# One pair of PSUM banks shared by decoded words and attention in the first group of a fused attention and expert kernel

## The chip, the cores and the metric

The kernel runs on one core of a Trainium2 chip. A core has five engines that run side by side and wait for each other by semaphores: TensorE (PE in the profile; PEld is its loading of weights), VectorE (DVE), ScalarE (ACT), GpSimd (POOL) and SyncE (SP, which here issues transfers). Matrix products land in PSUM, a small memory of banks; everything else is worked on in SBUF. The metric is the device time of one execution in microseconds (us), as the median of three runs.

## The reference

Three blocks follow each other. Chunks of 64 positions attend to themselves; the result, 4608 rows of 512, goes through a dense layer pair with `h - tanh(h)`; then each row is sent to two of eight experts, whose outputs are weighted and added.

```
scores = scale * q_c @ k_c.T        # chunks of 64, per head
attn   = exp(scores - max) / (sum + 1e-9)
x      = attn @ v_c                 # -> 4608 x 512
h = x @ w_in ; x = (h - tanh(h)) @ w_out          # 512 -> 2048 -> 512
top2 of x @ w_gate + log1p(exp(x @ w_noise)) * noise
out += weight * (max(x @ w1[e], 0) @ w2[e])       # for both experts of a row
```

The weights `w_in` and `w_out` reach the kernel as 64-bit floats, which the chip reads as pairs of 32-bit words; they have to be turned into 32-bit floats first. All other inputs are 32-bit floats.

## The kernel before

**Tiles and groups.** The rows are 36 tiles of 128, in nine groups of four. Group g's dense layer takes 16 steps (f = 0 to 15). A step is one block of layer 1 (`hp`, line 338, 12 matmuls of 128x512) and one block of layer 2 (`acc`, line 446, 12 matmuls), the latter a step behind, so the TensorE alternates `hp(f)`, `acc(f-1)`. Between blocks there are slots, two to a step: slot 2f stands behind `hp(f)`, slot 2f+1 behind `acc(f-1)`. Slots hold everything else in a list that is filled before (`at(h, fn)`), and what is in one slot is issued in the order in which it was put there: attention first, then the work on weights. Every engine works its own instructions strictly in that order.

**Attention of a tile** goes through scores (`s_mm`, 16 matmuls of 64x64), a maximum and a difference on the VectorE (`mx`, `e`), the exponential on the ScalarE, a sum and a reciprocal (`sm`, function `u_e`) with a multiplication, a transposition by the TensorE (`u_t`, `pt`), products with v (`p_mm`), and a split of the result in two parts, `xt` (ScalarE, then VectorE). The multiplication is done by the GpSimd for tiles below 8 and by the VectorE for the others (line 187). While group 0 runs its dense layer, the four tiles of group 1 (tiles 4 to 7) are attended to in its slots; from group 1 on the tiles of the next group, in "visits" that each transpose one tile, multiply the one before and score the one after (`u_attn`).

**Decoding.** In group 0 alone, the weights are still being prepared: in slot 2f the block of `w_in` for step f+2, in slot 2f+1 that of `w_out` for step f+1. The VectorE makes each in three instructions (lines 307, 313, 315) over a half-finished word, `word`, that is kept in PSUM; the third writes `x` to SBUF. Then the ScalarE and the GpSimd split `x` into `wa` or `wb`.

**PSUM.** Two banks are `hp` (and `pt`), four are `acc`, and two are left. Before, while decoding runs, one of the two is `word` and the other is `one`; `one` holds the scores or the products of a tile. The 16 matmuls of a tile are of two halves (`c`), and `u_s_chunk` and `u_p_chunk` do half a tile, 8 matmuls, in a slot of its own. At the end of group 0 (`decoded`) the two banks become `pair`, of shape [128, 2, 512]; a whole tile's scores lie in half 1 of both banks (columns 256 to 511) and products in half 0.

Of the kernel before, what the change touches and what calls it, by code (L numbers as in the profile page):

```python
# [31 lines left out]
def moe_chain_kernel(ctx: ExitStack, tc: tile.TileContext, q, k, v, w_in, w_out, wgn, noise,  # L32
# [27 lines left out]

    early, decoding = ExitStack(), ExitStack()
    ep = early.enter_context(tc.tile_pool(name="ep", bufs=1, space=PSUM))
    pairs = [ep.tile([128, 2, 512], F32, name=f"pair{i}") for i in range(3)]
    pools = {}
# [2 lines left out]
    def first_step():  # L69
        early.close()  # L70
        pools["acc"] = ctx.enter_context(tc.tile_pool(name="ap", bufs=1, space=PSUM))
        pools["two"] = decoding.enter_context(tc.tile_pool(name="gp", bufs=1, space=PSUM))

    def decoded():
        decoding.close()
        pools["two"] = ctx.enter_context(tc.tile_pool(name="qp", bufs=1, space=PSUM))
        pools["pair"] = pools["two"].tile([128, 2, 512], F32, name="pair")

    def after(what, n):
        turn[what] += 1  # L80
# [31 lines left out]
    def load_q(i):  # L112
        Q[i] = spare("wa", NF1 - 2)[:, i % 2] if 2 <= i < GS[0] else blk("q", "q", 2)
        nc.sync.dma_start(Q[i], q[i])
# [17 lines left out]
    def place_of(i, half):  # L132
        banks = pairs[after("early", 3)] if i < GS[0] else pools["pair"]
        return banks[:, :, 256 * half:256 * half + 256].rearrange("p c (a t) -> p c a t", a=4)
# [3 lines left out]
    def products(out, lhs, rhs, chunks=(0, 1)):  # L138
        for h in range(0, 8, 2):
            for c in chunks:  # L140
                rows = slice(64 * c, 64 * c + 64)
                for o in range(2):
                    cols = slice(64 * h + 64 * o, 64 * h + 64 * o + 64)
                    nc.tensor.matmul(out[64 * o:64 * o + 64, c, h // 2, :], lhsT=lhs[rows, cols],  # L144
                                     rhs=rhs[rows, cols], start=True, stop=True,
                                     tile_position=(64 * c, 64 * o))
# [53 lines left out]
        nc.scalar.copy(PT[i], pt)  # L200

    def p_mm(i):
        PX[i] = place_of(i, 0)
        products(PX[i], V.pop(i), PT.pop(i))
        if GS[0] <= i + 2 < NT:
            load_v(i + 2)
# [16 lines left out]
        p_lo(i)  # L223

    def one_bank():
        p = pools["two"].tile([128, 512], F32, name="one", bufs=1)
        return p.rearrange("p (c a t) -> p c a t", c=2, a=4)

    def u_s_chunk(i, c):
        if c == 0:
            PS[i] = one_bank()
            MX[i] = sp.tile([128, 2, 4, 1], F32, name="mx", bufs=2)
            Et[i] = sp.tile([128, 8, 64], F32, name="e", bufs=2)
        products(PS[i], Q[i], K[i], (c,))
        ps, mx = PS[i][:, c], MX[i][:, c]
        nc.vector.reduce_max(mx, ps, axis=AX.X)
        nc.vector.tensor_tensor(Et[i].rearrange("p (a c) t -> p c a t", c=2)[:, c], ps,
                                mx.to_broadcast([128, 4, 64]), op=ALU.subtract)  # L240
        if c == 1:
            for d in (Q, K, PS, MX):
                d.pop(i)
            load_q(i + 2)
            load_k(i + 2)

    def u_p_chunk(i, c):
        if c == 0:
            PX[i] = one_bank()
        products(PX[i], V[i], PT[i], (c,))  # L250
        g, j = place[i]
        if i == G0[g] and c == 0:
            XT[g] = new_xt(g, 128 * GS[g])
        s0 = j * 128 + 64 * c
        hi, lo = [XT[g][:, b, :, s0:s0 + 64] for b in range(2)]
        nc.scalar.copy(hi, PX[i][:, c])
        nc.vector.tensor_tensor(lo, PX[i][:, c], hi.bitcast(F32), op=ALU.subtract)
        if c == 1:
            for d in (V, PT, PX):
                d.pop(i)  # L260
            load_v(i + 2)

    def u_attn(old, mid, new):
        for t, fn in ((mid, u_t), (old, p_mm), (new, s_mm), (old, p_split), (new, s_max),
# [29 lines left out]
    def decode(raw, early=False, half=False):  # L294
        if raw.dtype == F32:
            return None if half else raw
        raw = raw.rearrange("p (m s) -> p m s", s=2)
        lo, hi = raw[:, :, 0], raw[:, :, 1]

        if early:  # L300
            part = pp.tile([128, 512], U32, name="word", tag="hp", bufs=2)
        else:
            if "two" in pools:
                part = pools["two"].tile([128, 512], U32, name="word", bufs=1)
            else:
                part = pairs[2][:, 0].bitcast(U32)
        nc.vector.tensor_scalar(part, lo, 29, None, op0=ALU.logical_shift_right)
        return part if half else decode_rest(raw, part)

    def decode_rest(raw, part):  # L310
        hi = raw[:, :, 1]
        x = blk("x", "y", 4, U32)
        nc.vector.scalar_tensor_tensor(part, hi, 3, part, op0=ALU.logical_shift_left,  # L313
                                       op1=ALU.bitwise_or)
        nc.vector.scalar_tensor_tensor(x, hi, 0x80000000, part, op0=ALU.bitwise_and,
                                       op1=ALU.bitwise_or)
        return x.bitcast(F32)

# [728 lines left out]
    def at(h, fn, *a):  # L1047
        slots[h].append(L(fn, *a))

    for i, hs in zip(range(GS[0], sum(GS[:2])), ((2, 3, 4, 5, 8, 15, 17), (5, 6, 7, 8, 11, 19, 20),  # L1050
                                                 (9, 11, 12, 13, 18, 22, 24),
                                                 (12, 14, 15, 16, 21, 26, 28))):
        at(hs[0], u_s_chunk, i, 0)
        at(hs[1], u_s_chunk, i, 1)
        at(hs[2], u_x, i)
        at(hs[3], u_e, i)
        at(hs[4], u_t, i)
        at(hs[5], u_p_chunk, i, 0)
        at(hs[6], u_p_chunk, i, 1)

    n0 = sum(GS[:2])
    visits = []
    at(H1, decoded)
    for g in range(1, NG - 1):
        hs = (1, 5, 9, 13, 18, 24) if g == 1 else (5, 9, 13, 24)
        for h in hs:
            visits.append((H1 * g + h, n0 if n0 < NT else None))
            n0 += 1  # L1070
    flow = [None, None]
    for h, i in visits:
        at(h, u_attn, *flow, i)
        if i:
            at(h + 1, u_x, i)
            at(h + 2, u_e, i)
        flow = [flow[1], i]

    for g in range(NG):
        h0 = H1 * g  # L1080
        at(h0, load_nz, g)
        if g > 0:
            n = GS[g - 1]
            for j in range(n):
                i = G0[g - 1] + j
                at(h0 + 1 + j, u_z, i)
                at(h0 + 5 + j, u_yt, i)

            if g == NG - 1:
                hs = (9, 11, 12, 13, 15, 17, 17, 19, 20, 23)  # L1090
            elif g == 1:
                hs = (9, 13, 14, 16, 17, 19, 21, 21, 22, 24)
            else:
                hs = (9, 13, 14, 16, 17, 18, 19, 20, 20, 24)
            for h, fn in zip(hs, (u_lg, u_gate, u_gate2, u_gate2h, u_gate2a, u_gate2b, u_gate2m,
                                  u_gate2c, u_gate3, u_pos)):
                at(h0 + h, fn, g - 1)
        if g == 0:
            at(26, store_consts)
            for o, f in ((0, 3), (1, 2), (1, 3)):  # L1100
                at(0, fetch_w, o, f)
            for f in range(NF1):
                at(2 * f, fetch_w, 0, f + 4)
                at(2 * f, prep_w, 1, f)
                at(2 * f, decode_w, 0, f + 2)
                at(2 * f, rebias_w, 0, f + 3)
                at(2 * f + 1, fetch_w, 1, f + 4)
                at(2 * f + 1, prep_w, 0, f + 2)
                at(2 * f + 1, decode_w, 1, f + 1)
                at(2 * f + 1, rebias_w, 1, f + 2)  # L1110
        else:
            for f in range(0, NF1):
                if g == 1:
                    if f < E:
                        at(h0 + 2 * f, zero_x, 2 * f)
                        at(h0 + 2 * f, zero_x, 2 * f + 1)
                    if f == E:
                        at(h0 + 2 * f, zero_rows, xs[SEAL - 128:SEAL, :])
                elif (g - 2) * NF1 + f < NT + DUMMY // 128:
                    at(h0 + 2 * f, zero_out, (g - 2) * NF1 + f)  # L1120
        if g == NG - 1:
            at(h0 - 4, u_cum)
            at(h0 - 2, u_bump)
            at(h0 + 12, load_list0)
            for c in range(min(3, SEAL // 128)):
                at(h0 + 8 + 3 * c, fetch_x, 0, c)
            for c in range(g0[1]):
                at(h0 + min(21 + 4 * c, H1 - 1), first_xt, c)
            for f in range(NF2):
                at(h0 + 2 * f + 7, fetch_e, 0, f)  # L1130
                at(h0 + 2 * f + 10, prep_e, 0, f)
# [128 lines left out]
```

## Time and profile before

| | us |
|---|---|
| median of 3 runs (1706.42 to 1706.70) | 1706.59 |
| the profiled execution itself | 1707.0 |
| its span, first to last instruction | 1705.2 |
| TensorE busy in the span | 1690.2 (99%) |
| VectorE busy | 773.8 (45%) |
| ScalarE busy | 529.6 (31%) |
| GpSimd busy | 493.5 (29%) |

The busy time of an engine is a sum over its instructions; the shares are means over stages that differ. Group 0's dense layer lies between 20 and 122 us of the span, and there the VectorE is far busier than in the mean. Rows of a timeline give the start, the duration, the engine, the line, the instruction, the tiles (output, arrow, inputs), their shapes and the number of instructions merged into the row; a bracket at the end gives the idle time of the engine ahead of it and what ended it. A 64x64 matmul in 32-bit floats makes two rows of the trace, so that half a tile reads x16 and a whole tile x32. The end of a matmul is modelled, and rows overlap a little; starts are the safer reading.

### The profile page before, as it was taken

How to read it: one execution, taken by the hardware profiler on the slowest of the kernel's cores; microseconds unless marked ns; L12 is line 12 of the kernel's file. 1: busy time of each engine (PE TensorE's matmuls, PEld its weight loads, DVE VectorE, ACT ScalarE, POOL GpSimd, SP SyncE). 2: the span in 40 equal slices, each digit the busy share in tenths (PEclk: the TensorE clock that was granted, in tenths of full speed). 3: DMA queues.
4: the chain of work that ended last, by engine and by line, in shares of the span. 5: the costliest groups of instructions: out<-in, count | busy, mean ns of one | idle time of the engine just before them, and what ended most of it. 6: DMA issues, size and time to landing. Idle time of an engine off the chain costs nothing.

```text
span 1705.2 us, 27189 instructions
## 1 busy us (share of the span) xinstructions
PE 1690.2 (99%) x10325; PEld 1422.1 (83%) x10326; DVE 773.8 (45%) x1909; ACT 529.6 (31%) x1036; POOL 493.5 (29%) x741
## 2 busy tenths in 40 slices
PE   8999999999999999999999999999999999999998
PEld 5778888888888888888888889888898888988887
DVE  8965645453545545443546333434333333343321
ACT  5653323222323232222333323323223222232211
POOL 4650130404031230404164523222232222232112
PEclk9999999999999999999999999999999999999999
DMA  7626352735323131313354543543344353443323
GB/s 297 217 90 188 98 160 62 207 81 170 104 94 105 70 112 43 126 32 114 91 164 124 149 104 82 112 104 72 93 101 105 75 96 86 99 101 80 72 26 38
DMA packets 198595, 185.18 MB, mean 109 GB/s; under 512 B 80928, under 2 KB 140320, under 8 KB 198432
## 3 DMA queue, kind: packets, MB, share of 16 engines
q1 hardware_dynamic: 176512, 138.80, 27.3%
q0 software_dynamic: 19328, 39.41, 11.9%
q10 hardware_dynamic: 2592, 4.72, 0.9%
q8 instruction: 111, 1.82, 0.5%
q14 instruction: 52, 0.43, 0.1%
HBM read 118.76 MB, written 64.10 MB: 107 GB/s over the span
## 4 chain that ended last, share of the span: by engine, by line
PE 97%; DVE 1%; ACT 1%; issue 0%; another core or an unknown queue 0%; POOL 0%; POOLq 0%; DVEq 0%; ACTq 0%
PE hp L338 47%; PE acc L446 46%; PE pair L144 2%; PE pt L198 1%; PE one L144 1%; PE hp L523 0%; PE hp L823 0%; POOL out_dram L797 0%; DVE sm L180 0%; DVE e L164 0%; DVE word L313 0%; DVE g L377 0%; PE hp L541 0%; DVE mx L157 0%
## 5 line engine op out<-in xcount | busy, mean ns | idle before, releaser
L338 PE MATMUL hp<-xt,wa 128*128 128x512 f32 (+5 forms) x4032 | 855.0, 361 | 1.2 <-ACT xt L214 0.9
L446 PE MATMUL acc<-wb,gt 128*128 128x512 f32 x3432 | 839.0, 391 | 0.6 <-ACT y L493 0.5
L338 PEld LDWEIGHTS hp<-xt,wa 128*128 128x128 f32 x4032 | 705.9, 188 | 111.8 <-issue 3.1
L446 PEld LDWEIGHTS acc<-wb,gt 128*128 128x128 f32 x3432 | 637.3, 188 | 129.7 <-ACT y L493 0.9
L385 DVE SCALAR_TENSOR_TENSOR gt<-hp,gt 128x384 fp32r<-128x384 f32 (+2 forms) x184 | 109.2, 594 | 430.3 <-ACT gt L382 418.1
L382 ACT ACTIVATE gt<-hp 128x384 fp32r<-128x384 f32 (+2 forms) x184 | 95.7, 520 | 439.4 <-PE hp L338 406.2
L377 DVE TENSOR_TENSOR g<-hp,g 128x512 f32<-128x512 f32 x144 | 99.5, 691 | 239.3 <-ACT g L374 216.9
L374 ACT ACTIVATE g<-hp 128x512 f32<-128x512 f32 x144 | 86.1, 598 | 366.4 <-PE hp L338 344.7
L323 POOL TENSOR_TENSOR wb<-st,wb 128x512 fp32r<-128x512 f32 x64 | 92.5, 1446 | 303.4 <-ACT wb L321 297.6
L403 POOL COPY spacer<-mark 1x1 f32<-1x1 f32 x181 | 47.4, 262 | 352.5 <-DVE mark L398 261.6
L797 POOL DMA_INDIRECT out_dram<-o,lsa x73 | 118.1, 1618 | 51.5 <-DVE o L794 29.1
L380 DVE TENSOR_TENSOR gt<-g,gt 128x512 fp32r<-128x512 f32 x128 | 88.9, 694 | 87.9 <-ACT gt L378 72.1
L378 ACT CAST gt<-g 128x512 fp32r<-128x512 f32 x144 | 89.4, 621 | 110.4 <-DVE g L377 92.1
L616 POOL TENSOR_SCALAR r<-d 128x4 f32<-128x4 f32 x9 | 4.5, 495 | 376.4 <-ACT d L607 376.3
L667 POOL DMA_INDIRECT xs<-yr,row x72 | 73.1, 1015 | 31.7 <-issue 23.4
L276 DVE TENSOR_TENSOR xt<-xg,xt 128x512 fp32r<-128x512 f32 x80 | 54.5, 681 | 54.1 <-ACT xt L275 52.2
L275 ACT CAST xt<-xg 128x512 fp32r<-128x512 f32 x80 | 48.8, 610 | 97.1 <-DVE xg L499 85.7
L667 POOL DMA_INDIRECT lst<-pay,row x72 | 71.3, 990 | 21.1 <-issue 20.0
L499 DVE STREAM_TRANSPOSE xg<-xg 128x512 f32<-128x512 f32 x80 | 56.3, 704 | 2.5 <-DMA xg<-xs 2.5
L323 DVE TENSOR_TENSOR wa<-st,wa 128x512 fp32r<-128x512 f32 x64 | 44.0, 688 | 0.1
L219 DVE TENSOR_TENSOR xt<-pair,xt 128x512 fp32r<-128x512 f32 x32 | 22.1, 689 | 41.1 <-ACT xt L214 41.1
L321 ACT CAST wb<-st 128x512 fp32r<-128x512 f32 x64 | 39.6, 619 | 0.1
(189 smaller groups left out, 884.8 us busy)
## 6 DMA issues: line engine op xcount, KB each, us to landing
st<-in_w_dram SPq DMA_DIRECT2D x112, 256.0 KB
xg<-xs SPq DMA_DIRECT2D x320, 64.0 KB
out_dram<-zero SPq DMA_DIRECT2D x40, 256.0 KB
x2d<-y SPq DMA_DIRECT2D x36, 256.0 KB
z<-x2d SPq DMA_DIRECT2D x144, 64.0 KB
yr<-x2d SPq DMA_DIRECT2D x36, 256.0 KB
q<-in_q_dram SPq DMA_DIRECT2D x34, 256.0 KB
vs<-in_v_dram SPq DMA_DIRECT2D x34, 256.0 KB
```

Of the source, the lines that this page charges most:

```text
L323: eng.tensor_tensor(w[:, 1, :], x, w[:, 0, :].bitcast(F32), op=ALU.subtract)
L338: nc.tensor.matmul(s.hp[:, :n], lhsT=w[:, a, d, :], rhs=s.xt[:, b, d, :n], start=(i == 0), stop=(i == 11))
L374: nc.scalar.activation(g, hp[:, :n], AF.Tanh)
L377: nc.vector.tensor_tensor(g, hp[:, :n], g, op=ALU.subtract)
L378: nc.scalar.copy(hi, g)
L380: eng.tensor_tensor(lo, g, hi.bitcast(F32), op=ALU.subtract)
L382: nc.scalar.activation(hi, hp[:, :n], AF.Relu)
L385: nc.vector.scalar_tensor_tensor(lo, hp[:, :n], 0.0, hi.bitcast(F32), op0=ALU.max, op1=ALU.subtract)
L446: nc.tensor.matmul(s.grp["acc"][j][:m], lhsT=s.gt[:, a, j * 128:j * 128 + m], rhs=s.B[s.f][:, b, :], start=(s.f == 0 and i == 0), stop=(s. ...
L499: nc.vector.transpose(out=out.rearrange("p b (g c) -> p g b c", g=4), in_=x.rearrange("p (g b r) -> p g b r", g=4, b=4))
L667: s = nc.gpsimd.indirect_dma_start(out=to, out_offset=bass.IndirectOffsetOnAxis(ap=at, axis=0), in_=src, in_offset=None)
L797: a = nc.gpsimd.indirect_dma_start(out=out, out_offset=bass.IndirectOffsetOnAxis(ap=en[:m, 0:1], axis=0), in_=o[:m], in_offset=None, compu ...
```

## The change

There is one pool for the two banks from the end of the first attention on, and one tile in it, `pair`. While decoding runs, the words lie in half 0 of both banks, as [128, 2, 256] in place of [128, 512] in one bank. Tiles 4 to 7 have both their scores and their products in half 1, at different times; from tile 8 on products are in half 0 as before. Group 0's attention is done by whole tiles: six scores (tiles 4 to 9, so two more than before) in slots 2, 6, 12, 18, 24 and 30, from the second on with a transposition ahead of them, and four products in slots 9, 15, 21 and 27. Group 1 then has four visits in place of six. Some of the work on the gates of group 0's tiles, done in group 1, moves by up to two slots.

```diff
-    early, decoding = ExitStack(), ExitStack()
+    early = ExitStack()
...
-        pools["two"] = decoding.enter_context(tc.tile_pool(name="gp", bufs=1, space=PSUM))
-
-    def decoded():
-        decoding.close()
-        pools["two"] = ctx.enter_context(tc.tile_pool(name="qp", bufs=1, space=PSUM))
-        pools["pair"] = pools["two"].tile([128, 2, 512], F32, name="pair")
+        two = ctx.enter_context(tc.tile_pool(name="qp", bufs=1, space=PSUM))
+        pools["pair"] = two.tile([128, 2, 512], F32, name="pair")
...
     def p_mm(i):
-        PX[i] = place_of(i, 0)
+        PX[i] = place_of(i, 1 if GS[0] <= i < sum(GS[:2]) else 0)
...
-    def u_s_chunk(i, c):
...
-    def u_p_chunk(i, c):
...
-            if "two" in pools:
-                part = pools["two"].tile([128, 512], U32, name="word", bufs=1)
-            else:
-                part = pairs[2][:, 0].bitcast(U32)
+            part = pools["pair"][:, :, 0:256].bitcast(U32)
+            lo = lo.rearrange("p (c m) -> p c m", c=2)
...
-    for i, hs in zip(range(GS[0], sum(GS[:2])), ((2, 3, 4, 5, 8, 15, 17), (5, 6, 7, 8, 11, 19, 20),
-                                                 (9, 11, 12, 13, 18, 22, 24),
-                                                 (12, 14, 15, 16, 21, 26, 28))):
-        at(hs[0], u_s_chunk, i, 0)
-        at(hs[1], u_s_chunk, i, 1)
...
-        at(hs[4], u_t, i)
-        at(hs[5], u_p_chunk, i, 0)
-        at(hs[6], u_p_chunk, i, 1)
...
-    n0 = sum(GS[:2])
+    n0 = GS[0]
     visits = []
-    at(H1, decoded)
+    for a in range(GS[1] + 2):
+        visits.append((2 + 6 * a - min(2 * a, 2), n0))
+        n0 += 1
     for g in range(1, NG - 1):
-        hs = (1, 5, 9, 13, 18, 24) if g == 1 else (5, 9, 13, 24)
+        hs = (5, 9, 13, 24)
...
     for h, i in visits:
-        at(h, u_attn, *flow, i)
+        if h < H1:
+            if flow[0]:
+                at(h - 3, p_mm, flow[0])
+                at(h - 3, p_split, flow[0])
+            at(h, u_attn, None, flow[1], i)
+        else:
+            at(h, u_attn, *flow, i)
...
-            elif g == 1:
-                hs = (9, 13, 14, 16, 17, 19, 21, 21, 22, 24)
```

The TensorE's order in the first steps of group 0, from slot 2 on, in the kernel before (`one` is the bank of half tiles, `pt` a transposition):

```order
L144 MATMUL one<-ks,q 64x64 x8
L446 MATMUL acc<-wb,gt 128x512 x12
L144 MATMUL one<-ks,q 64x64 x8
L338 MATMUL hp<-xt_323,wa 128x512 x12
L446 MATMUL acc<-wb,gt 128x512 x12
L144 MATMUL one<-ks,q 64x64 x8
L338 MATMUL hp<-xt_323,wa 128x512 x12
L144 MATMUL one<-ks,q 64x64 x8
L446 MATMUL acc<-wb,gt 128x512 x12
L338 MATMUL hp<-xt_323,wa 128x512 x12
L198 MATMUL pt<-ident,e 128x128 x4
```

The same place now:

```order
L140 MATMUL pair<-ks,q 64x64 x16
L407 MATMUL acc<-wb,gt 128x512 x12
L299 MATMUL hp<-xt_323,wa 128x512 x12
L407 MATMUL acc<-wb,gt 128x512 x12
L299 MATMUL hp<-xt_323,wa 128x512 x12
L194 MATMUL pt<-ident,e 128x128 x4
L140 MATMUL pair<-ks,q 64x64 x16
L407 MATMUL acc<-wb,gt 128x512 x12
L299 MATMUL hp<-xt_323,wa 128x512 x12
L407 MATMUL acc<-wb,gt 128x512 x12
L140 MATMUL pair<-pts,vs 64x64 x16
```

Four half tiles in slots 2, 3, 5 and 6 are now two whole ones in slots 2 and 6, and a whole tile's products stand in slot 9.

The VectorE in slots 8 and 9 of group 0 before, with the semaphores that each instruction waits for (`word` is the half-finished word, `wa_83` the raw block of `w_in` for step 6):

```order
L377 TENSOR_TENSOR g<-hp,g 128x512 [waits Activation_49]
L398 MEMSET mark 1x1
L180 TENSOR_REDUCE sm<-e 128x8
L184 TENSOR_SCALAR sm<-sm 128x8 [waits DVE_49]
L185 RECIPROCAL sm<-sm 128x8 [waits DVE_49]
L307 TENSOR_SCALAR word<-wa_83 128x512 [waits DMAHW1_49]
L313 SCALAR_TENSOR_TENSOR word<-wa_83,word 128x512 [waits DVE_49]
L315 SCALAR_TENSOR_TENSOR x<-wa_83,word 128x512 [waits DVE_49]
L238 TENSOR_REDUCE mx<-one 128x4 [waits PE_49]
```

The same place now:

```order
L338 TENSOR_TENSOR g<-hp,g 128x512 [waits Activation_49]
L359 MEMSET mark 1x1
L176 TENSOR_REDUCE sm<-e 128x8
L180 TENSOR_SCALAR sm<-sm 128x8 [waits DVE_49]
L181 RECIPROCAL sm<-sm 128x8 [waits DVE_49]
L265 TENSOR_SCALAR pair<-wa_83 128x2x256 [waits DMAHW1_49]
L274 SCALAR_TENSOR_TENSOR pair<-wa_83,pair 128x2x256 [waits DVE_49]
L276 SCALAR_TENSOR_TENSOR x<-wa_83,pair 128x512 [waits DVE_49]
L215 TENSOR_TENSOR xt_761<-pair,xt_761 128x2x4x64 [waits Activation_49]
```

The words are now written to and read from `pair`, and behind them stands the second part of tile 4's split in place of half of tile 6's scores.

The TensorE in slot 9 now, with its waits, from the layer-2 block ahead of it to the first matmul behind it (`vs` is v, `pts` the transposed exponentials):

```order
L407 MATMUL acc<-wb,gt 128x512 [waits Activation_49]
L407 MATMUL acc<-wb,gt 128x512 x3
L407 MATMUL acc<-wb,gt 128x512 [waits Pool_49]
L407 MATMUL acc<-wb,gt 128x512 x7
L140 MATMUL pair<-pts,vs 64x64 [waits DMAHW5_49,DVE_49]
L140 MATMUL pair<-pts,vs 64x64 x15
L299 MATMUL hp<-xt_323,wa 128x512 [waits PE_49,Activation_49]
```

The products in `pair` wait for a transfer of v and for the VectorE. In the built program the count that they wait for is the one that `x<-wa_83,pair` of slot 8 brings, the last row but one of the VectorE above; each of the other whole tiles in group 0's slots waits in the same way for the last `x` of the slot ahead of its own (the first, in slot 2, for that of slot 1).

## Rows read from the trace of the kernel before

**Rows 1.** Page, part 4: shares of the chain that ended last.

```profile
PE 97%; DVE 1%; ACT 1%; issue 0%; another core or an unknown queue 0%; POOL 0%; POOLq 0%; DVEq 0%; ACTq 0%
```

**Rows 2.** Windows in group 0: PE, PEld, DVE, ACT, POOL busy, clock, DMA.

```profile
34.00:60.00 26.00, 26.00 (x170) 20.68 (x169) 24.83 (x49) 16.30 (x29) 17.87 (x15) 1.00 0.58 201
60.00:122.00 62.00, 62.00 (x402) 49.01 (x401) 48.51 (x91) 35.42 (x65) 36.46 (x30) 1.00 0.47 157
```

**Rows 3.** Timeline, TensorE: a half tile alone, in group 0.

```profile
97.69 2.88 PE L338 MATMUL hp<-xt,wa 128*128 128x512 f32 x12
100.50 0.68 PE L144 MATMUL one<-pts,vs 64*64 64x64 f32 x16
...
103.97 2.88 PE L338 MATMUL hp<-xt,wa 128*128 128x512 f32 x12
```

**Rows 4.** Timeline, TensorE: start of group 1, its first two visits.

```profile
121.97 2.88 PE L338 MATMUL hp<-xt,wa 128*128 128x512 f32 x12
124.69 2.88 PE L446 MATMUL acc<-wb,gt 128*128 128x512 f32 x12
127.50 0.69 PE L144 MATMUL pair<-ks,q 64*64 64x64 f32 x32
...
130.98 2.88 PE L446 MATMUL acc<-wb,gt 128*128 128x512 f32 x12
...
136.42 2.89 PE L446 MATMUL acc<-wb,gt 128*128 128x512 f32 x12
139.14 0.60 PE L198 MATMUL pt<-ident,e 128*128 128x128 f32 x4
139.67 0.69 PE L144 MATMUL pair<-ks,q 64*64 64x64 f32 x32
...
143.17 2.88 PE L446 MATMUL acc<-wb,gt 128*128 128x512 f32 x12
```

**Rows 5.** Timeline, TensorE: slots 2 and 3 of group 0.

```profile
26.36 0.68 PE L144 MATMUL one<-ks,q 64*64 64x64 f32 x16
...
31.35 0.68 PE L144 MATMUL one<-ks,q 64*64 64x64 f32 x16 [1.31 <-DVE e L239]
```

**Rows 6.** Timeline, VectorE: last decoding instruction of slot 1.

```profile
29.20 0.69 DVE L315 SCALAR_TENSOR_TENSOR x<-wb,word 128x512 uint32<-128x512 uint32 x1
```

**Rows 7.** Timeline, all engines: tile 4's sum and the decoding of slot 8.

```profile
49.50 0.68 DVE L180 TENSOR_REDUCE sm<-e 128x8 f32<-128x512 f32 x1
...
50.55 0.67 DVE L307 TENSOR_SCALAR word<-wa 128x512 uint32<-128x512 uint32 x1
...
51.99 0.69 DVE L315 SCALAR_TENSOR_TENSOR x<-wa,word 128x512 uint32<-128x512 uint32 x1
```

**Rows 8.** Timeline, all engines: from a layer-1 block to its `g`.

```profile
58.02 3.04 PE L338 MATMUL hp<-xt,wa 128*128 128x512 f32 x12
...
61.16 0.60 ACT L374 ACTIVATE g<-hp 128x512 f32<-128x512 f32 x1 [1.64 <-PE hp L338]
61.79 0.69 DVE L377 TENSOR_TENSOR g<-hp,g 128x512 f32<-128x512 f32 x1 [0.62 <-ACT g L374]
```

**Rows 9.** Tile `pair`, whole span: count, ns minimum/median/maximum, first and last start.

```profile
L157 DVE TENSOR_REDUCE mx<-pair x32: 639/681/692, 6.9 to 728.5; 128x8 f32<-128x512 f32 x32
L164 DVE TENSOR_TENSOR e<-pair,mx x32: 679/692/692, 7.6 to 729.2; 128x512 f32<-128x512 f32 x32
L214 ACT CAST xt<-pair x32: 567/587/592, 15.0 to 772.6; 128x512 fp32r<-128x512 f32 x32
```

**Rows 10.** Timeline, all engines: products, scores and split in a visit of group 1.

```profile
165.52 0.69 PE L144 MATMUL pair<-pts,vs 64*64 64x64 f32 x32
...
166.03 0.65 PE L144 MATMUL pair<-ks,q 64*64 64x64 f32 x32
...
166.75 0.59 ACT L214 CAST xt<-pair 128x512 fp32r<-128x512 f32 x1 [0.54 <-PE pair L144]
```

**Rows 11.** Windows at the end, columns as in rows 2.

```profile
1698.00:1700.00 2.00, 0.00 (x0) 0.00 (x0) 0.00 (x0) 0.64 (x1) 1.09 (x1) 1.00 0.00 0
1700.00:1705.20 5.20, 0.00 (x0) 0.00 (x0) 0.00 (x0) 0.00 (x0) 0.47 (x1) 0.50 0.43 50
```

**Rows 12.** Timeline, TensorE: its first matmuls in the kernel.

```profile
1.30 4.45 PE L823 MATMUL hp<-warm 128*128 128x512 bf16 x10 [1.30 <-DVE warm L817]
5.68 1.75 PE L144 MATMUL pair<-ks,q 64*64 64x64 f32 x64
7.37 1.47 PE L823 MATMUL hp<-warm 128*128 128x512 bf16 x6
```

## Prediction before the run

> **What bounds the kernel now.** I read the chain of waits first: 97% of it is TensorE [rows 1], so what the change is worth is TensorE time plus whatever makes the TensorE stand. Then windows over group 0, the only dense layer in which order or placement change much. There the TensorE has no gap, but from 34 to 60 us the VectorE is busy for 24.83 of 26.00 us, and for 48.51 of 62.00 after that [rows 2]: a second engine close behind the first. Then the timeline for the price of each insertion, and at last the order for who waits for whom.
>
> **TensorE work that goes.** A block of 12 matmuls takes 124.69 - 121.97 = 2.72 us [rows 4]. A half tile alone between two blocks costs 103.97 - 97.69 - 2 x 2.72 = 0.84 us [rows 3]; a whole tile alone 130.98 - 124.69 - 5.44 = 0.85 us, and a transposition with a whole tile's scores 143.17 - 136.42 - 5.44 = 1.31 us [rows 4]. Half a tile costs what a whole one does.
>
> From slot 2 to the end of group 0 the kernel before takes 121.97 - 26.36 = 95.61 us [rows 4, 5]. Of that 29 blocks are 78.88 and one wait is 1.31 [rows 5]; 15.42 are left, which is 16 halves at 0.84 (13.44) and four transpositions at 0.50. After the change group 0 holds five whole tiles alone (the scores in slot 2, four products) at 0.85 and five transpositions with scores at 1.31: 10.80. That is 4.6 us less. In group 1 the first two of six visits go, a whole tile alone and one with a transposition: 0.85 + 1.31 = 2.16 less. From group 2 on each tile is in the slot it was in. TensorE work: -6.8 us.
>
> **Waits that come.** All ten insertions in group 0 now wait until the VectorE has finished decoding in the slot ahead, since words and tile share `pair`. That a wait on `pair` does not tell its halves apart is to be seen before: in a visit the products (half 0) start at 165.52 and take 0.69, yet their split starts at 166.75, behind the scores (half 1) that start at 166.03 [rows 10].
>
> Slot 2: the TensorE was there at 26.36 [rows 5]; the last `x` of slot 1 ends at 29.20 + 0.69 = 29.89 [rows 6]. Wait 3.5 us. The 1.31 us wait in slot 3 goes with its half tile.
>
> For the others I lay out the VectorE. Decoding a block takes 51.99 + 0.69 - 50.55 = 2.13 us (2.15 with the wait of the next), a tile's sum and reciprocal 50.55 - 49.50 = 1.05 [rows 7]; `g` is done 61.79 + 0.69 - 61.06 = 1.42 us after its layer-1 block ends (58.02 + 3.04) [rows 8]; maximum and difference take 1.37, the ScalarE's split 0.59, and the VectorE's, of the same size as the difference, 0.69 [rows 9].
>
> Slot 6: scores at 29.9 are done at 30.5; maximum and difference until 31.9, slots 2 and 3 decoded at 36.2. `hp(2)` ends at 29.9 + 0.85 + 2 x 2.72 = 36.2, `g` at 37.6, sum at 38.65, slots 4 and 5 decoded at 42.95. The TensorE has done `acc(1)`, `hp(3)` and the transposition at 42.1. Wait 0.85.
>
> Slots 9, 15, 21, 27 (products): behind `hp(f)` the VectorE does `g`, a tile's sum and the decoding of the even slot, 1.42 + 1.05 + 2.15 = 4.62; the TensorE has only `acc(f-1)`, 2.72. Wait 1.9, three times. In slot 26 the sum is tile 8's, whose multiplication is the VectorE's too (0.69, priced as a difference of that shape [rows 9]): wait 2.6 in slot 27. Behind the waiting products stands the next `hp`, and for it the VectorE's next `g`; the VectorE itself stands for about 1.3 us until products and the ScalarE's split are there.
>
> Slots 12, 18, 24, 30 (scores): counted from the start of the products, the VectorE has split at 2.0, decoded at 4.15, `g` at 5.0, and two more blocks at 9.3; the TensorE gets there at 0.85 + 3 x 2.72 + 0.50 = 9.5. No wait, with 0.2 to spare.
>
> Waits: 3.5 + 0.85 + 5.7 + 2.6 = 12.65, less the 1.31 that goes: +11.3 us. With the work: +4.5 us.
>
> **The clock.** [...] No row shows what a fall costs in mid-kernel. Below: nothing, if the VectorE's pace hides a slow block. Above: at the start the first ten matmuls take 4.45 us and six of the same size, later, 1.47, so the clock rose between 1.30 + 4.45 and 7.37, at most 6.1 us after the first [rows 12]; as long a stretch at half speed loses 3.0 us. I take the middle, 1.5, for each of the two, since `g` waits for `hp` and a slow `hp` can't all be hidden: +3.0 us.
>
> [...]
>
> **Sum.** +4.5 + 3.0 = +7.5 us on the profiled execution's 1707.0: 1714.5. That execution lies 0.4 above the median of 1706.59, so the forecast is 1714.1 us. New operands in two pieces ([128, 2, 256] for [128, 512]) I cost at nothing, as operands of 2x4x64 in `pair` take 0.692 [rows 9], like the words' 0.69 [rows 7]; a loss of 0.05 on each of the 29 decodings in the slots would be 1.5 us of the VectorE's time.
>
> **Rivals.**
> 1. The waits come, the clock stays. For it: nothing but the end of the trace shows a fall. 1706.6 + 4.5 = 1711.1.
> 2. The clock falls at the 1.9 us waits as well: three more at 1.5, 1718.6. Against it: 1.9 is less than the 2 us of the trace's end.
> 3. The VectorE is ahead of my table, because it stands less often once the halves of tiles are gone (four instructions on halves become two on a whole tile). With half of the waits (6.3), -6.8 - 1.3 + 6.3 = -1.8: 1704.8. Against it: from 34 to 60 us the VectorE has 5% of its time free [rows 2].
> 4. The wait does not reach to the words, tiles and words in the two halves run side by side, and TensorE work alone counts: -6.8 - 1.3 = -8.1: 1698.5. This is faster than before. It would decide from the point where the TensorE is at slot 2 and starts its scores at 26.4, not 29.9. Against it: the counts in the built program, and rows 10.
>
> [...]
>
> **How the numbers follow.** Forecast 0.45, rival 1 0.25, rival 2 0.12, rival 3 0.13, rival 4 0.05. The forecast's own range, with falls at 0 to 3.0 each, is 1711 to 1717. For 8 in 10 I take 1707.5 to 1718.5: rival 4 and the faster half of rival 3 lie below it, part of rival 2 above. About 0.2% (3.4 us) is what a measurement here tells from no change, so "slower" begins at 1710.0 and "faster" ends at 1703.2. Slower: nearly all of the forecast (0.44), three quarters of rival 1 (0.19), rival 2 (0.12), a little of rival 3 (0.01): 0.76. Faster: rival 4 and a quarter of rival 3: 0.08. Same: 0.16.
>
> **What would show it.** The TensorE's timeline of the changed kernel: the first scores in `pair` of group 0 at about 29.9 us with an idle time of 3.5 ahead and an `x` as its releaser; four products each with 1.9 to 2.6; scores without a wait but for slot 6's; group 0 ending about 7 us later than at 121.97 without a fall and 10 us with two (11.3 - 4.6, + 3.0) and group 1 about 2 us shorter. The granted clock in a window around 31 to 36 us tells the forecast from rival 1, one just behind the first products (about 54 to 60 us) rival 2. I am wrong if the first scores start near 26.4, if the waits sum to less than 9 us, or if anything past group 1 changes its length.

## The result, and the profile after

The changed kernel takes 1714.91 us (median of 6 runs, 1714.68 to 1716.28) against 1706.51 for the kernel before (6 runs, 1706.24 to 1706.76): 1.0051 times as long, 95% interval 1.0038 to 1.0064. That is slower, by 8.4 us, where 1714.1 was forecast. Its profiled execution took 1716.28 us with a span of 1714.6, so it lies 1.4 above its own median.

The first view to read is again the TensorE's timeline, from the layer-1 block ahead of slot 2 to group 2 (start, duration, engine, line, instruction, tiles, array and shape, count; in the bracket the idle time ahead and what ended it):

```profile
30.49 1.13 PE L140 MATMUL pair<-ks,q 64*64 64x64 f32 x32 [3.57 <-issue]
31.55 5.07 PE L407 MATMUL acc<-wb,gt 128*128 128x512 f32 x12
36.46 2.91 PE L299 MATMUL hp<-xt,wa 128*128 128x512 f32 x12
...
46.19 0.69 PE L140 MATMUL pair<-ks,q 64*64 64x64 f32 x32 [0.93 <-DVE x L276]
...
49.67 2.88 PE L299 MATMUL hp<-xt,wa 128*128 128x512 f32 x12
...
57.12 0.69 PE L140 MATMUL pair<-pts,vs 64*64 64x64 f32 x32 [1.85 <-DVE x L276]
57.74 3.04 PE L299 MATMUL hp<-xt,wa 128*128 128x512 f32 x12
60.62 2.88 PE L407 MATMUL acc<-wb,gt 128*128 128x512 f32 x12
...
66.59 0.69 PE L140 MATMUL pair<-ks,q 64*64 64x64 f32 x32
...
119.90 0.69 PE L140 MATMUL pair<-pts,vs 64*64 64x64 f32 x32 [3.37 <-DVE x L276]
120.52 4.61 PE L299 MATMUL hp<-xt,wa 128*128 128x512 f32 x12
124.97 2.90 PE L407 MATMUL acc<-wb,gt 128*128 128x512 f32 x12
...
134.47 2.88 PE L299 MATMUL hp<-xt,wa 128*128 128x512 f32 x12
...
229.75 2.88 PE L299 MATMUL hp<-xt,wa 128*128 128x512 f32 x12
```

The kernel before, at the start of group 2:

```profile
219.40 2.88 PE L338 MATMUL hp<-xt,wa 128*128 128x512 f32 x12
```

Slot 2 answers to [rows 5]: the scores that started at 26.36 now wait 3.57 us. Slot 6 waits 0.93; slots 12 and on (66.59) have scores without a wait; the products of slots 9, 15 and 21 wait 1.85, 1.85 and 1.84 (the first is shown), those of slot 27 3.37. Group 1 begins at 134.47 where it began at 121.97 [rows 4]; group 2 begins at 229.75, in the kernel before at 219.40. The releaser of slot 2 reads "issue", that is, the profile names none. That it is the last `x` of slot 1 shows in the VectorE's timeline, which answers to [rows 6]; here with slot 26 and the GpSimd's rows below it:

```profile
29.70 0.69 DVE L276 SCALAR_TENSOR_TENSOR x<-wb,pair 128x512 uint32<-128x512 uint32 x1
...
115.96 1.28 POOL L341 TENSOR_TENSOR gt<-g,gt 128x512 fp32r<-128x512 f32 x1 [1.88 <-ACT gt L339]
...
116.31 1.47 DVE L184 TENSOR_TENSOR e<-e,sm 128x512 f32<-128x512 f32 x1
117.19 1.73 POOL L284 TENSOR_TENSOR wb<-x,wb 128x512 fp32r<-128x512 f32 x1
...
119.16 0.69 DVE L276 SCALAR_TENSOR_TENSOR x<-wa,pair 128x512 uint32<-128x512 uint32 x1
```

The first `x` ends at 30.39 and the scores start at 30.49; the last one ends at 119.85 and the products start at 119.90. Ahead of it tile 8's multiplication (line 184) took 1.47 us. It started while an instruction of the GpSimd was running, and ended 0.54 us behind that one's end (117.78 and 117.24); the GpSimd's next instruction, which started beside it, took 1.73 us where the one before took 1.28.

All waits of the TensorE from 18 to 135 us, by line and releaser (total, times, longest):

```profile
PE pair L140 <- DVE x L276: 9.8, 5, 3.4
PE pair L140 <- issue: 3.6, 1, 3.6
...
```

These two are the change's, 13.4 us together; the line left out is the wait ahead of group 0's first block (1.1 us), which the kernel before has as well (0.9).

Windows over the waits (start:end, length, busy time and count of PE, PEld, DVE, ACT, POOL, then granted clock, DMA share, GB/s):

```profile
15.50:18.90 3.40, 3.40 (x60) 2.62 (x63) 3.32 (x6) 1.53 (x3) 1.04 (x1) 0.50 1.04 409
29.20:36.00 6.80, 5.51 (x43) 4.46 (x44) 5.84 (x10) 3.71 (x8) 3.83 (x4) 0.50 0.42 137
54.00:62.00 8.00, 6.15 (x57) 4.80 (x56) 6.19 (x11) 3.99 (x7) 4.83 (x4) 1.00 0.44 134
121.30:124.70 3.40, 3.40 (x9) 2.64 (x8) 2.75 (x4) 1.06 (x2) 1.29 (x1) 0.50 0.21 77
```

The granted clock is 0.50 from 29.2 to 36.0 us, that is over the end of slot 2's wait and the block behind it. It is 0.50 again from 121.3 to 124.7, beginning 1.4 us after the TensorE had started again in slot 27, and 1.00 behind the 1.85 us of slot 9. In the kernel before it is 1.00 over all of group 0 ([rows 2] from 34 us on). In the slow stretches the twelve matmuls of a block take 5.07 and 4.61 us and not 2.9.

There is a third slow stretch, from 15.5 to 18.9 us, ahead of group 0. The kernel before has none there, although its TensorE waits in the same way (1.14 us ahead of a transposition, 1.15 in the changed kernel):

```profile
15.50:18.90 3.40, 2.56 (x72) 1.95 (x72) 3.26 (x8) 2.30 (x6) 1.44 (x2) 1.00 1.03 407
```

### The profile page after: what moved, and what is told of

It reads as the page before. It is cut to its first block, busy times and chain, and to the rows that moved or that the text cites. A ratio compares the mean times of both kernels' runs of the same rounds, so it can differ in the third digit from the quotient of the medians.

```text
span 1714.6 us, 27181 instructions
## 1 busy us (share of the span) xinstructions
PE 1688.0 (98%) x10325; PEld 1422.7 (83%) x10326; DVE 775.1 (45%) x1897; ACT 530.0 (31%) x1032; POOL 494.8 (29%) x741
```

## The experiments

The theory: the loss is made where the TensorE has to wait for decoding because words and tiles share `pair`, and behind the two longest of these waits the clock falls. The main rival: it is the schedule by whole tiles that costs, with fewer and later insertions, and the placement only happens to be there. Two sizes were open besides: what a fall costs, and why slot 27 waited 3.37 and not 2.6. Each kernel was timed in turn with the kernel before on the same chip.

**Placement without the schedule.** The kernel before, its half tiles in their slots, with `word` in half 0 and `one` in half 1 of `pair`.

```diff
-        p = pools["two"].tile([128, 512], F32, name="one", bufs=1)
-        return p.rearrange("p (c a t) -> p c a t", c=2, a=4)
+        return pools["pair"][:, :, 256:512].rearrange("p c (a t) -> p c a t", a=4)
...
-                part = pools["two"].tile([128, 512], U32, name="word", bufs=1)
+            part = pools["pair"][:, :, 0:256].bitcast(U32)
+            lo = lo.rearrange("p (c m) -> p c m", c=2)
```

> The kernel before with the placement alone changed: words in half 0 of `pair`, half tiles in half 1 of it, in the slots and with the halves of the kernel before; group 1 with six visits. Theory: sixteen halves now wait for the decoding of the slot ahead, with waits of about 3.4, 0.9, 0.9, 1.5, 1.4, 2 and 0.8 us, 11 to 13 us in all in place of 1.3, plus one or two falls of the clock (1.5 to 2.6 each): 1717 to 1722 us, the slowest of all. Rival (placement costs nothing and the schedule by whole tiles brings the waits): 1706 to 1708 us.

It took 1720.37 us, 1.0085 (1.0069 to 1.01). The TensorE's waits from 18 to 139 us:

```profile
PE pair L140 <- DVE x L311: 9.1, 14, 1.8
PE pair L140 <- issue: 3.6, 1, 3.6
```

Fifteen of the sixteen half tiles wait, in the order of before. So the placement brings the waits without the new schedule, and it costs more so: the whole tiles win back a part. In group 0 the clock fell twice here, behind the wait of 3.57 us (0.54 over 30 to 36 us) and behind one of 1.85:

```profile
89.22 0.68 PE L140 MATMUL pair<-pts,vs 64*64 64x64 f32 x16 [1.85 <-DVE x L311]
89.83 4.61 PE L334 MATMUL hp<-xt,wa 128*128 128x512 f32 x12
```

The granted clock is 0.57 over 90 to 94 us.

**The new schedule without the shared banks.** The words stay in SBUF; scores and products keep `pair`.

```diff
-        if early:
-            part = pp.tile([128, 512], U32, name="word", tag="hp", bufs=2)
-        else:
-            part = pools["pair"][:, :, 0:256].bitcast(U32)
-            lo = lo.rearrange("p (c m) -> p c m", c=2)
+        part = pp.tile([128, 512], U32, name="word", tag="hp", bufs=2) if early else lo
```

> The changed kernel with the half-finished words kept in SBUF, in place of the raw low words, and not in `pair`; the order of attention is the changed one. Theory: no insertion in group 0 waits for a decoding, so TensorE work alone counts (-6.8 us) and the 1.31 us wait in slot 3 goes: 1698 to 1701 us, with no idle over 1.5 us in group 0. Rival (the waits come from doing whole tiles, not from the shared tile): 1711 to 1715 us, waits in the same slots. A third outcome: the decoding gets slower with both operands in SBUF while GpSimd works there (the multiplication of tile 8 took 1.47 us beside GpSimd and 0.69 without), 1703 to 1720 us, with the VectorE's three instructions at well over 0.69 us.

It took 1729.28 us, 1.0142 (1.0126 to 1.0157): slower than any of the three outcomes allowed, though the third names the cause. The TensorE's timeline in slot 2 and at tile 4's products:

```profile
25.49 0.69 PE L140 MATMUL pair<-ks,q 64*64 64x64 f32 x32
...
55.15 0.69 PE L140 MATMUL pair<-pts,vs 64*64 64x64 f32 x32
```

No insertion waits any more for decoding, so the waits on `pair` did come from the words in it. But of the TensorE's waits from 18 to 150 us the largest is now one for weights:

```profile
PE acc L403 <- POOL wb L280: 13.4, 8, 2.5
```

The timeline of VectorE and GpSimd says why:

```profile
54.09 0.42 DVE L261 TENSOR_SCALAR wb<-wb 128x512 uint32<-128x512 uint32 x1
54.55 0.69 DVE L270 SCALAR_TENSOR_TENSOR wb<-wb 128x512 uint32<-128x512 uint32 x1
...
58.50 1.35 DVE L261 TENSOR_SCALAR wa<-wa 128x512 uint32<-128x512 uint32 x1
59.53 1.22 POOL L184 TENSOR_TENSOR e<-e,sm 128x512 f32<-128x512 f32 x1
...
60.71 1.71 POOL L280 TENSOR_TENSOR wb<-x,wb 128x512 fp32r<-128x512 f32 x1
61.33 1.64 DVE L272 SCALAR_TENSOR_TENSOR x<-wa 128x512 uint32<-128x512 uint32 x1
```

From 22 to 150 us a decoding instruction whose operands all lie in SBUF takes 1.05 to 1.67 us when it starts while the GpSimd is at work, and 0.42 or 0.69 when it starts alone. In the first case it ends 0.55 us (line 261: 0.28) behind the GpSimd's instruction, as the last row does (62.97 and 62.42). With the word in PSUM the second and the third instruction take 0.69 us, also where they start while the GpSimd is at work, as the groups of the tile `pair` in the changed kernel show (count, ns minimum/median/maximum, first and last start):

```profile
L274 DVE SCALAR_TENSOR_TENSOR pair<-wa,pair x14: 695/695/697, 26.7 to 118.4; 128x512 uint32<-128x512 uint32 x14
L276 DVE SCALAR_TENSOR_TENSOR x<-wa,pair x14: 686/686/689, 27.5 to 119.2; 128x512 uint32<-128x512 uint32 x14
```

The experiment shows what the waits hang on, but it does not price them.

**Products a slot earlier.** They go from behind the odd slot's block to the even slot (`h - 4`), where they stand ahead of that slot's decoding and need only the decoding of the slot before.

```diff
-                at(h - 3, p_mm, flow[0])
-                at(h - 3, p_split, flow[0])
+                at(h - 4, p_mm, flow[0])
+                at(h - 4, p_split, flow[0])
```

> The changed kernel with group 0's four products (and their splits) one slot earlier, in slots 8, 14, 20 and 26, ahead of that slot's decoding. Theory (the TensorE waits for the last decoding on `pair` in the slot ahead): in front of an even slot that decoding is `w_out`'s of the odd slot, which the VectorE finishes before g; the four waits of 1.85 to 3.37 us (8.9 in all) go, and the clock's fall behind slot 27 (about 1.6) with them, while slots 2 and 6 still wait 3.5 and 0.9 and the fall in slot 2 stays (about 2.6). 1714.9 - 8.9 - 1.6 = 1704 to 1708 us. Rival (the VectorE is simply too slow for whole tiles in group 0, wherever they stand): the waits move to other blocks, 1713 to 1716 us.

It took 1705.85 us against 1705.11 in the same rounds, 1.0004 (0.9995 to 1.0013): no difference to the kernel before. Its TensorE in slots 2, 8 and 14:

```profile
30.28 1.13 PE L140 MATMUL pair<-ks,q 64*64 64x64 f32 x32 [3.58 <-issue]
...
52.60 0.69 PE L140 MATMUL pair<-pts,vs 64*64 64x64 f32 x32 [0.34 <-issue]
...
71.74 0.69 PE L140 MATMUL pair<-pts,vs 64*64 64x64 f32 x32 [0.42 <-DVE x L276]
```

The waits of the products go from 1.85 to 0.34 and 0.42 (0.45 and 0.52 in slots 20 and 26). Sharing the banks is not the cost as such; it is what the VectorE still has ahead of it when a tile comes.

**The wait of slot 2 filled with work.** 13 matmuls of 128x512 that no one uses, ahead of the scores, in the changed kernel.

```diff
+    def fill(n):
+        p = pools["acc"].tile([128, 512], F32, name="acc", bufs=4)
+        for _ in range(n):
+            nc.tensor.matmul(p, lhsT=WI[0][:, 0, 0:128], rhs=WI[0][:, 0, :], start=True, stop=True)
+
+    at(2, fill, 13)
```

> The changed kernel with 13 extra matmuls of 128x512 (about 2.95 us) into a free accumulator bank in front of tile 4's scores in slot 2, where the TensorE otherwise stands for 3.57 us; their output is used by nobody. Theory (the long wait brings the clock down, and that is paid on top): the clock stays at 1.00 there, the layer-2 block behind takes 2.9 us and not 5.07, and the time falls by 2 to 2.6 us to 1712.0 to 1713.0, although TensorE does more. Rival (the slow blocks are hidden behind the VectorE's pace): within 0.5 us of the changed kernel, 1714.4 to 1715.4. If the extra matmuls run over the wait they would make it slower, above 1715.4.

It took 1713.36 us, 1.0041 (1.0028 to 1.0055). A second timing of the changed kernel, on another chip, gave 1716.45, 1.0053 (1.004 to 1.0067):

> The changed kernel itself, on the chip and in the rounds of the next three, as their yardstick (the kernel before took 1705.1 us on the chip of the runs above and 1706.5 in the first result). Every theory: its ratio to the kernel before as in the first result, 1.0051, so 1713 to 1715 us where before takes 1705 to 1706.5.

The intervals of the two overlap. In the profile the block behind slot 2 is fast again, and the TensorE's timeline shows where one is slow instead:

```profile
29.87 0.69 PE L140 MATMUL pair<-ks,q 64*64 64x64 f32 x32 [0.57 <-DVE x L276]
30.50 3.03 PE L407 MATMUL acc<-wb,gt 128*128 128x512 f32 x12
...
43.06 0.69 PE L140 MATMUL pair<-ks,q 64*64 64x64 f32 x32 [0.94 <-DVE x L276]
...
53.99 0.93 PE L140 MATMUL pair<-pts,vs 64*64 64x64 f32 x32 [1.84 <-DVE x L276]
54.85 4.34 PE L299 MATMUL hp<-xt,wa 128*128 128x512 f32 x12
```

The window over it, columns as above:

```profile
54.00:58.00 4.00, 4.00 (x40) 3.25 (x41) 2.24 (x4) 1.71 (x3) 2.38 (x2) 0.57 0.52 150
```

The wait of 1.84 us in slot 9, behind which the changed kernel kept its clock at 1.00, here has 0.57 behind it, and the block takes 4.34 us. So a wait of that length goes either way, and what was rival 2 does occur. For the price of the fall in slot 2 the medians are inconclusive. The profiles give one: from the scores of slot 2 to those of slot 6 the TensorE needs 43.06 - 29.87 = 13.19 us here and 46.19 - 30.49 = 15.70 in the changed kernel, 2.5 more.

**The same work in slot 2, with the products a slot earlier.** The two edits above together; no products' wait is left that could bring the clock down.

> Products one slot earlier (as in the first experiment, 1.0004 of the kernel before) and the 13 extra matmuls in slot 2. No wait over 1 us is left in group 0. Theory (a fall of the clock in slot 2 costs about 2.3 us there, and falls need a long wait): no fall in group 0, 2 to 2.5 us less than with products alone, 1702.8 to 1704 where the kernel before takes 1705.1, ratio 0.9985 to 0.9993. Rival (the slow blocks in slot 2 are hidden): ratio 1.000 to 1.001.

1705.40 us against 1706.45, 0.9990 (0.9981 to 0.9999). With the products earlier, filling slot 2 moves the ratio from 1.0004 to 0.9990, by some 2.4 us, give or take 2 (each ratio is known within 0.0009). The filling takes the place of idle time, and in the profile the clock is 1.00 all through group 0; so this is about what the fall in slot 2 costs. From the scores of slot 2 to those of slot 6 the two profiles differ by 2.4 us as well, 15.60 and 13.18.

**Tile 8's multiplication on the GpSimd.** The changed kernel, with one tile more on that engine.

```diff
-        eng = nc.gpsimd if i < sum(GS[:2]) else nc.vector
+        eng = nc.gpsimd if i < sum(GS[:2]) + 1 else nc.vector
```

> The changed kernel with tile 8's multiplication by the reciprocal done by GpSimd, as for tiles 4 to 7, in place of the VectorE. Theory (in slot 26 it is this instruction, at 1.47 us beside GpSimd's work and not the 0.69 that the prediction took, that makes the wait in slot 27 3.37 us and not 1.85): that wait becomes 1.8 to 1.9, as in slots 9, 15 and 21, and the fall of the clock behind it becomes rarer; 1.5 to 3 us less than the changed kernel, 1711 to 1713. Rival (slot 27 waits for something else, such as GpSimd's split of the weights): the wait stays over 3 us and the time within 0.5 us; if GpSimd gets late by the added 1.3 us, transpositions or blocks wait for it, and nothing is won.

1712.78 us, 1.0037 (1.0023 to 1.005), against 1.0053 for the changed kernel in the same rounds. The timeline of slot 27:

```profile
117.23 1.04 POOL L184 TENSOR_TENSOR e<-e,sm 128x512 f32<-128x512 f32 x1
...
118.41 0.69 PE L140 MATMUL pair<-pts,vs 64*64 64x64 f32 x32 [1.85 <-DVE x L276]
```

And the window behind it:

```profile
119.00:125.00 6.00, 6.00 (x34) 4.97 (x27) 4.92 (x9) 3.43 (x6) 2.60 (x3) 1.00 0.15 44
```

The wait is that of the other products, 1.85, and the clock stays at 1.00 behind it. In the profile both the surplus of 1.52 us and the fall in slot 27 go with that one instruction. The two intervals overlap, but the spans of the profiled executions, 1714.8 and 1711.6 us, differ by those two terms.

**All scores later.** Scores in slots 3, 8, 14, 20, 26 and 31. The products stand four slots ahead of a later tile's scores, by the edit above (`h - 4`), and so come in slots 10, 16, 22 and 27.

```diff
-        visits.append((2 + 6 * a - min(2 * a, 2), n0))
+        visits.append(((3,8,14,20,26,31)[a], n0))
```

> Products one slot ahead of the odd slot as in the first experiment, and scores in slots 3, 8, 14, 20, 26 and 31 in place of 2, 6, 12, 18, 24 and 30. Theory (the first scores wait for the last decoding of the slot ahead, which the VectorE reaches 2.2 us later than in slot 2, while the TensorE has a block of 2.72 us more to do): the first wait falls from 3.58 to about 2.7 us and the one in slot 6 goes; 1 to 2.5 us less than the first experiment, depending on whether the clock still falls at 2.7 us: ratio 0.9990 to 1.0000. Rival (the wait in slot 2 is the VectorE's backlog from the start, and comes back wherever the scores stand): ratio 1.0000 to 1.0010.

1706.96 us, 1.0003 (0.9994 to 1.0012): nothing is to be seen of the 1 to 2.5 us that it should have won over the products a slot earlier (1.0004). The first scores, in the TensorE's timeline:

```profile
31.39 1.13 PE L140 MATMUL pair<-ks,q 64*64 64x64 f32 x32 [2.58 <-DVE x L276]
32.46 4.08 PE L299 MATMUL hp<-xt,wa 128*128 128x512 f32 x12
```

And the window over them:

```profile
30.00:36.00 6.00, 4.61 (x43) 3.79 (x44) 4.50 (x7) 2.22 (x4) 3.75 (x3) 0.72 0.35 87
```

A block later the wait is 2.58 us in place of 3.58, since the VectorE is behind there too, and the clock falls all the same, to a mean of 0.72 in this window.

**The first scores ahead of the decoding.** Products a slot earlier, and tile 4's scores moved from slot 2 to a place ahead of group 0's first block.

```diff
     prep_w(0, 1)
+    u_attn(None, None, GS[0])
     decode_w(1, 0)
...
-            at(h, u_attn, None, flow[1], i)
+            if i > GS[0]:
+                at(h, u_attn, None, flow[1], i)
```

> Edit: as e1 (products a slot earlier, in even slots), and besides the scores of tile 4 leave slot 2 and are issued ahead of group 0's first layer-1 block, before the first word of w_out is decoded into pair; their maximum and difference on the VectorE then stand ahead of that decoding. Theory (what is left of the change's cost in e1 is the 3.6 us wait in slot 2 and the fall of the clock behind it): no scores in slot 2, no long wait there, granted clock 1.00 from 26 to 122 us; what comes instead is the 1.37 us of maximum and difference ahead of the decoding, by which the first layer-2 block gets its weights later, in two or three waits of 0.5 to 2 us. Group 0 ends 1 to 3 us earlier than in e1; 1702.5 to 1705 us, 0.997 to 0.9995 of the kernel before. Rival (the delay of the weights costs what the scores' wait did): one wait of 3 us or more at the first layer-2 block, clock down again, 1705 to 1707.5.

1704.49 us against 1706.29, 0.9991 (0.9982 to 1.0). The waits of its TensorE from 18 to 125 us:

```profile
PE pair L140 <- DVE xt L215: 1.8, 1, 1.8
PE pair L140 <- DVE x L276: 1.7, 1, 1.7
PE pair L140 <- issue: 1.5, 4, 0.4
...
```

With two shorter ones for weights that is 6.0 us in place of 14.5, each with the wait ahead of group 0's first block. No wait is over 1.8 us, and the clock was 1.00 from 20 to 125 us. This kernel and the one with earlier products and the filled slot are the only ones below the kernel before, by 0.1%, with intervals that end at no difference. No kernel here got more than that out of sharing the banks.

## Why the prediction held, step by step

**TensorE work, -6.8 us: right.** In group 0 the change spends 134.47 - (30.49 - 3.57) = 107.55 us from its arrival at slot 2, against 95.61 before, +11.94. Of it 13.41 - 1.31 = 12.10 are waits and 4.06 falls of the clock (below), which leaves -4.2 for the work where -4.6 was forecast. Group 1 goes from 219.40 - 121.97 = 97.43 to 229.75 - 134.47 = 95.28 us: -2.15, forecast -2.16.

**Waits, +11.3: right, each in its place, 0.8 short in sum.** Forecast and measured: slot 2 3.5 and 3.57, slot 6 0.85 and 0.93, three products 1.9 and 1.85, scores none and none. Slot 27 is the mis-sized term: 2.6 and 3.37. I priced the multiplication by a difference of its shape, 0.69 [rows 9], but that one has an operand in PSUM, and the multiplication has none: alone, in group 1, it takes 0.69 too, but beside the GpSimd it took 1.47. The multiplication moved to GpSimd shows the rest of the table right, 1.85 for 1.9.

The 1.47 us, and the 1.41 to 1.65 of the two-input instructions that met the GpSimd between 54 and 66 us with the words in SBUF, have their end in common: each lies 0.54 or 0.55 us behind that of the GpSimd instruction. Line 261 has one input; at 58.50 it took 1.35 us in place of 0.42 and ended 0.28 us behind. What makes them wait no run shows. The difference by which I priced the multiplication, on PSUM, took 0.69 us at most [rows 9] and has no such wait in it.

**The clock, +3.0: right in place, 1.1 short in size.** The sum has two falls, for the two waits that were longer than the 2.00 us for which the TensorE stands at 1.00 in [rows 11] ahead of its 0.50: slot 2 (3.5) and slot 27 (2.6). In group 0 the clock fell there and nowhere else. That 2 us are a limit was my estimate, and no run shows one: behind the waits of 2.58 to 3.58 us it fell in every profile, and behind some of 1.84 to 2.52 too. What a fall cost, from the start of an insertion to the second block behind it: slot 2 36.46 - 30.49 = 5.97 against 49.67 - 46.19 = 3.48 in slot 6, so 2.5 us; slot 27 124.97 - 119.90 = 5.07 against 60.62 - 57.12 = 3.50, so 1.6. Forecast were 1.5 each, between 0 and 3.0. The 2.4 and 2.5 us of the filled slot agree with the first; the multiplication's move, 3.2 us in the spans, of which 1.5 is wait, agrees with the second. Twice 1.5 was the middle of the bounds; the fall of slot 27 has that size, and the one of slot 2 lasted twice as long, 6.8 us at the low clock and not 3.4.

**The sum: right by a little luck.** From slot 2 on, groups 0 and 1 together are 9.8 us longer in the profiled execution where 7.5 was forecast. (Group 0 alone ends 12.5 us later, 0.56 of it from ahead of slot 2; forecast were 10.) Two more differences lie between the two profiles, and no run ties either to the change. The changed kernel came to slot 2 0.56 us later (26.92 and 26.36), behind the slow stretch from 15.5 to 18.9 us. In the profiles of kernels that are the same up to slot 2, group 0 starts at 20.8 to 21.1 us with such a stretch and at 19.3 and 20.5 without one. Against that, 0.8 us went in the expert stage: the TensorE is 10.4 us late at what was 959 us of the kernel before and 9.6 late from 1084 on. There the profiled execution of the kernel before lost 0.2 us at 978 and 0.6 at 1075. None of the ten other profiles has the loss at 1075, not even the placement alone, which keeps the schedule of before. The prediction named a change past group 1 as a sign against it; this one lies in the execution that it is compared with.

Between the spans of the two profiles lie 9.4 us, between the medians 8.4: the changed kernel's median lies 1.4 below its profiled execution, and there lies the luck. The mean granted clock was 0.995 in the two longest of the six executions (1716.28 and 1716.08) and 0.996 or 0.997 in the other four (1714.68 to 1715.01). So most executions spent less time at the low clock than the profiled one; in which stretch is in no profile.

**Rivals.** Rival 1 (clock stays) is out by the windows. Rival 3 (VectorE ahead of the table) is out: the waits are the table's. Rival 4 (halves independent) is out: the scores started at 30.49, not 26.4, and without words in `pair` they start at 25.49 with no wait. The wait alone was not taken away, with words and tiles still in the same banks. Rival 2 (falls at 1.9 us waits) did not occur in the changed kernel's two profiles, but it did once each in the one with slot 2 filled and in the placement alone; its chance of 0.12 was no exaggeration.

## What to carry to other kernels

When two uses are put into one tile, list for each use what the other's engine has still queued when it arrives: the same shared banks cost 8.4 us or nothing that could be measured, by whether a tile's products stood behind or ahead of 2.15 us of decoding. A wait of the TensorE can cost 1.5 to 2.5 us more than itself: in group 0 those of 2.58 us and longer did so in every profile here, and some of those from 1.84 to 2.52 did. And price a VectorE instruction by one with its operands in the same memories and with the same neighbour on the GpSimd, not by its shape alone: the multiplication of tile 8 took 1.47 us where its shape had said 0.69.

## What the runs showed of the hardware that I had not expected

- The granted clock falls behind waits of 1.84 us in some executions and not in others: 1.00 in the changed kernel's windows of slot 9, 0.57 in the run with slot 2 filled, with the same wait ahead. It was so for other lengths too. With the words in SBUF, one wait of 2.52 us (ended at 62.48) had 0.57 behind it over 62 to 66 us, and eight matmuls took 3.69 us; another (ended at 87.36) had 1.00 over 86 to 92, and eight took 2.12. Ahead of group 0 a wait of 1.15 us had 0.50 behind it in the changed kernel and one of 1.14 had 1.00 in the kernel before. Waits of 2.58, 2.84, 3.37, 3.57 and 3.58 all had a fall behind them in the profiles.
- Beside GpSimd instructions the decoding with all its operands in SBUF (lines 261, 270 and 272 with the words in SBUF) went from 0.42 or 0.69 us an instruction to 1.05 to 1.67, and tile 8's multiplication from 0.69 to 1.47. With the word in PSUM lines 274 and 276 of the changed kernel took 0.686 to 0.697 us, beside the GpSimd or not.
